# The 15-product expert stage: input sums as a two-step pipeline, six of their steps beside the last triple of products, spaced loads and a new order of the tail

## The chip, the cores and the metric

One core of one Trainium2 chip runs the whole kernel. The metric is the device time of one execution in microseconds, lower is better. TensorE (PE) does the matrix products, VectorE (DVE) and ScalarE (ACT) the elementwise work, GpSimd (POOL) a part of it, and SyncE (SP) issues most of the DMA transfers. Each engine works through its own instructions in program order; semaphores tie them together.

## The reference, cut to what matters

```
for t in range(768):                      # attention, 4 x 8 heads of 48
    y[t]  = r[t] @ (state + (u*k[t]) outer v[t])
    state = w * state + k[t] outer v[t]
x = y as 3072 tokens x 384
h = maximum(maximum(x @ w1, x @ w2), x @ w3);  x = h @ w_out      # 768 wide
rms = sqrt(mean(x*x, axis=-1) + 1e-06);        xn = x / rms * rms_g
g = xn @ w_gate;  val = xn @ w_val                                 # 1536 wide
out = (silu(g) * val) @ moe2_w_out
```

## The kernel before, in words

Tokens are handled as six units of 512. Attention and the first expert layer run unit by unit and fill the first 400 us. The second expert layer, which the change is about, runs as three **passes** p = 0, 1, 2 over pairs of units. Every product in f32 is made of three matmuls on a high part and a low part of each operand (`mm3`, lines 98 to 100: high x high, high x low, low x high), so each operand has to be split: ACT copies the rounded high part, DVE or POOL subtracts it to get the low part.

For gate and value the kernel does not multiply 3 x 3 blocks of weights with 3 blocks of two units directly. It uses a scheme with 15 products on sums and differences of the blocks. The six blocks of a pair of units (a, b, c of the first, d, e, f of the second) are combined into 15 **input sums** by `form_steps(p)`, a generator; one `next` of it is one step. A step makes a sum on DVE (lines 708 and 710) in a buffer of the pool `sb`, splits it with an ACT copy (line 716) and a DVE subtraction (line 717), and leaves the two halves in `sets[i]`. The product i reads `sets[i]`, so the sums of the next pass may overwrite a set once the products of this pass that use it are done. Sums are needed in the order 2, 5, 7, 4, 3, 10, 12, ...

`PLAN` is a table for one **triple** (three of the 12 columns of 128 in the hidden layer): 30 products (`M i x`) and the work around them, with a due time for each. Four copies of it, one period apart, are sorted into one list for each pass, 120 products in all; n counts them. Kinds of entries: `e`, `E` copy a bank to `sb` (line 997), `p`, `c`, `v`, `C` combine banks (lines 999 and 1009), `s` is the Silu (984), `m` the gate times value (988, 990), `h` and `l` split a hidden column into a buffer `hb` (992, 995; there are three such buffers), `o` multiplies it into the output of the pass's first unit (`out_block`, nine matmuls in the three d). The hidden columns of the second unit stay in `h2`; `h_split(f)` splits them (lines 1070, 1071) and `second(f, d)` multiplies them (`b_out`). When an output is complete, `b_out` copies the bank into one of two `ob` buffers and stores it (lines 878, 879).

The order at the end of a pass before: the six `o` blocks that come behind the last product are put between the first blocks of `second`; `form_steps(p + 1)` starts there, one step for each f (and more behind block 20), and what is left of it runs behind the first nine products of the next pass. The last nine blocks of `second` are kept as `filler` for the start of the next pass. In pass 0, `stats_late` sums the squares of the last unit meanwhile.

Beside the products runs the generator `bg` (`behind(p + 1)`), one step per product from n = 25 on: it loads the next pair (`x2_load`, line 696), for the last pair does the Newton steps of 1/rms (lines 539 to 555, small tiles `n`), loads 1/rms to all partitions (`rb`, line 684) and normalises (line 689, six operations). In pass 0 alone every third product also has a weight chunk to make: SP loads three pieces `wsf` (line 650), ACT and POOL split them (655, 656), POOL's queue stores them (657); passes 1 and 2 load the finished chunks (660).

Of the kernel before, what the change touches and what calls it, by code (L numbers as in the profile page):

```python
# [9 lines left out]
F32 = mybir.dt.float32  # L10
F32R = mybir.dt.float32r
# [5 lines left out]
ALU = mybir.AluOpType  # L17
# [48 lines left out]
def r32(ap):  # L66
    return ap.bitcast(F32)
# [3 lines left out]
def rwkv_moe_kernel(ctx, tc, rkT, rkv, wd, ub, cst, rg, w1p, wo1p, w2p, out):  # L71
# [404 lines left out]
    hs, sB = {}, {}  # L476
# [57 lines left out]
    def newton_steps(p, pl):  # L534
        m, y, t = (pl.tile([128, 8], F32, tag=f"n{n}", name=f"n{n}{p}") for n in range(3))
        late = p == NB // 2 - 1
        if late:
            yield
        sync.dma_start(m, msd[p].rearrange("j (a b) -> (j a) b", b=8))
        for _ in range(3):  # L540
            yield
        dve.tensor_scalar(out=m, in0=m, scalar1=1.0 / DM, scalar2=1e-6, op0=ALU.mult, op1=ALU.add)
        dve.tensor_scalar(out=y.bitcast(U32), in0=m.bitcast(U32), scalar1=1, scalar2=0x7fffffff,
                          op0=ALU.logical_shift_right, op1=ALU.bitwise_xor)
        dve.tensor_scalar(out=y, in0=y, scalar1=1.8352577e-20, scalar2=None, op0=ALU.mult)
        dve.tensor_scalar(out=m, in0=m, scalar1=-0.5, scalar2=None, op0=ALU.mult)
        for n in range(4):
            if n == 2:
                yield
            dve.tensor_tensor(out=t, in0=y, in1=m, op=ALU.mult)  # L550
            dve.tensor_tensor(out=t, in0=t, in1=y, op=ALU.mult)
            dve.scalar_tensor_tensor(out=y, in0=t, scalar=1.5, in1=y, op0=ALU.add, op1=ALU.mult)
        if late:
            yield
        sync.dma_start(rsd[p].rearrange("j (a b) -> (j a) b", b=8), y)
# [23 lines left out]
    with tc.manual_schedule():  # L579
# [48 lines left out]
        plan = []  # L628
# [49 lines left out]
        def norm_steps(p):  # L678

            us = (2 * p, 2 * p + 1)  # L680
            x = [x2s.pop(u) for u in us]
            rb = sB["r"].tile([128, 2, 512], F32, tag="rb", name=f"rb{p}")
            for j in range(2):
                sync.dma_start(rb[:, j], rsd[p, j].partition_broadcast(128))
            for _ in range(4 if p else 1):
                yield
            for j in range(2):
                for k in range(3):
                    dve.scalar_tensor_tensor(out=x[j][:, k], in0=x[j][:, k], scalar=rg_sb[:, k:k + 1],
                                             in1=rb[:, j], op0=ALU.mult, op1=ALU.mult)  # L690
                    yield
                xr[us[j]] = x[j]

        def x2_load(u):
# [3 lines left out]
        def form_steps(p):  # L698

            one, two = xr.pop(2 * p), xr.pop(2 * p + 1)  # L700
            a, b, c = (one[:, k] for k in range(3))
            d, e, f = (two[:, k] for k in range(3))
            hold = {}

            def op(name, x, y, kind="add"):
                o = hold[name] = sb.pop(0)
                if kind == "neg":
                    dve.scalar_tensor_tensor(out=o, in0=x, scalar=-1.0, in1=y, op0=ALU.mult, op1=ALU.subtract)
                else:
                    dve.tensor_tensor(out=o, in0=x, in1=y, op=getattr(ALU, kind))  # L710
                return o

            def split(i, x, *drop):
                form_left[0] -= 1
                t = sets[i]
                act.copy(t[:, 0], x)
                dve.tensor_tensor(out=t[:, 1], in0=x, in1=r32(t[:, 0]), op=ALU.subtract)
                for name in drop:
                    sb.append(hold.pop(name))

            s = op("s", e, f, "subtract")
            m = op("m", b, s)
            yield
            split(2, op("t", m, c, "subtract"), "t")
            yield
            split(5, d)
            yield
            w = op("w", a, c, "subtract")
            v = op("v", w, d, "neg")
            yield  # L730
            split(7, op("t", f, v), "t")
            yield
            split(4, v, "v")
            yield
            split(3, op("t", a, d), "t")
            yield
            split(10, w)
            yield
            split(12, op("t", b, a, "subtract"), "t")
            yield  # L740
            split(6, op("t", w, s, "neg"), "t", "w")
            yield
            split(0, s, "s")
            yield
            split(11, op("t", e, d, "subtract"), "t")
            yield
            split(1, m, "m")
            yield
            split(9, f)
            yield  # L750
            split(13, b)
            yield
            split(14, c)
            yield
            split(8, op("t", b, e), "t")

        def set_tiles(t, n):
            for k in range(n):
# [3 lines left out]
        for u in range(NB):  # L762
# [14 lines left out]
            for n, sl in enumerate(slots):  # L777
# [29 lines left out]
                elif u == L:  # L807
                    if n == 0:
                        for v in range(2):
                            x2_load(v)  # L810
                        for _ in range(8):
                            sb.append(br.tile([128, 512], F32, tag="sb", bufs=8, name=f"sb{len(sb)}"))
# [95 lines left out]
        def stats_late():  # L908

            t = [sb.pop(0) for _ in range(3)]  # L910
            for k in range(3):
                sync.dma_start(t[k], x2d[NB - 1, :, k])
            for _ in range(8):
                yield
            for k in range(3):
                act.activation(t[k], t[k], AF.Square)
                if k:
                    pool.tensor_tensor(out=t[0], in0=t[0], in1=t[k], op=ALU.add)
                yield
            yield  # L920
            yield
            sr = br.tile([128, 2, 512], F32R, tag="rb", name="sr")
            hi, lo = sr[:, 0], sr[:, 1]
            act.copy(hi, t[0])
            yield
            dve.tensor_tensor(out=lo, in0=t[0], in1=r32(hi), op=ALU.subtract)
            yield
            yield
            ps = banks.pop(0)
            pe.matmul(ps, ones, hi, start=True, stop=False)  # L930
            pe.matmul(ps, ones, lo, start=False, stop=True)
            act.copy(t[0][0:1], ps[0:1])
            sync.dma_start(msd[NB // 2 - 1, 1:2], t[0][0:1])
            banks.append(ps)
            sb.extend(t)
# [3 lines left out]
        for p in range(NB // 2):  # L939
# [17 lines left out]
            def behind(p):  # L957

                for v in range(2 * p, 2 * p + 2):
                    x2_load(v)  # L960
                yield
                yield
                if p == NB // 2 - 1:
                    yield from newton_steps(p, br)
                yield from norm_steps(p)
# [51 lines left out]
            def out_block(g, f, d):  # L1017
                k = ("h", g, f)
                count[d] += 1
                b_out(3 * g + f, d, get(k), ac, count[d] == 1, count[d] == F2, 2 * p)  # L1020
                drop(k)

            n = 0
            for m, (_, _, kind, g, arg) in enumerate(plan):
                if kind == "M":
# [8 lines left out]
                    drop(("b", g, arg[1], root(arg[0])))  # L1034
                    n += 1
                    if n < 10:
                        next(fs, None)
                    if n >= 25:
                        next(bg, None)
# [13 lines left out]
                elif kind != "o":  # L1053
                    emit(kind, g, arg)
                elif m < last:
                    out_block(g, *arg)
                else:
                    tail.append((arg[0], arg[1], g))
            if more:
# [1 line left out]
            for _ in bg:  # L1061
                pass
            po2 = [banks.pop(0) for _ in range(3)]
            pr = {}
            fs = form_steps(p + 1) if more else iter(())
            late = stats_late() if p == 0 else iter(())

            def h_split(f):
                h = pr[f] = hs_free.pop(0)
                act.copy(h[0], h2[:, f])  # L1070
                dve.tensor_tensor(out=h[1], in0=h2[:, f], in1=r32(h[0]), op=ALU.subtract)  # L1071

            def second(f, d, p=p, po2=po2, pr=pr):
                b_out(f, d, pr[f], po2, f == 0, f == F2 - 1, 2 * p + 1)
                if d == 2:
                    hs_free.append(pr.pop(f))

            tail.sort()
            mix_in = {0: tail[:3], 2: tail[3:]}
            done = 0  # L1080
            for b in range(3 * F2 - (9 if more else 0)):
                f, d = divmod(b, 3)
                while done < F2 and done <= f + 2 and hs_free:
                    h_split(done)
                    done += 1
                second(f, d)
                for f, d, g in mix_in.get(b, ()):
                    out_block(g, f, d)
                next(late, None)
                if d == 0 or b > 20:  # L1090
                    next(fs, None)
            while done < F2:
                h_split(done)
# [185 lines left out]
```

## Time and profile before

| what | value |
|---|---|
| median of 3 runs | 869.72 us (868.94 to 872.7) |
| the profiled execution | 867.82 us, span 866.1 us |
| PE busy | 807.2 us, 93% |
| DVE / ACT / POOL busy | 580.6 / 427.3 / 249.9 us |
| granted TensorE clock, mean | 0.973 |
| chain that ended last | PE 67%, DVE 17%, ACT 6%, DMA 5% |

The span runs from the first to the last instruction of the profiled execution; its own time is 1.7 us longer, and 1.9 us under the median of the runs. Busy PE time is modelled and overlaps, so it does not show stalls well: the distance from one matmul's start to the next does.

### The profile page before, as it was taken

Reading aid. Unit: us, or ns where it says so; the run is one execution under the profiler, and the core shown is the slowest. Engines: PE = TensorE matmul, PEld = TensorE weight load, DVE = VectorE, ACT = ScalarE, POOL = GpSimd, SP = SyncE. Lnnn points to the kernel's source line nnn. Section 1 sums busy time; section 2 is a strip of 40 time slices with the busy share of each in tenths; the row PEclk is TensorE's granted clock in tenths of the full one; section 3 lists DMA queues with packets and bytes.
Section 4 is the critical chain, followed back from the end, with each engine's and each line's share of the span. In section 5 each row is a group of like instructions: output and inputs, shape, how many; then the busy total and the mean of one; then the engine's idle time right before and its main releaser. Section 6 shows DMA issues by size and latency. Waiting matters only on the chain.

```text
span 866.1 us, 14096 instructions
## 1 busy us (share of the span) xinstructions
PE 807.2 (93%) x5098; PEld 657.9 (76%) x5098; DVE 580.6 (67%) x940; ACT 427.3 (49%) x812; POOL 249.9 (29%) x242
## 2 busy tenths in 40 slices
PE   7799999999999999998969998788999879999985
PEld 6688878888888888886848886666788667888864
DVE  6999989688788585187455664766665485655531
ACT  1988955544545532235736663554444345444331
POOL 2588645434445320132646740100000000000000
PEclk8899999999999999999979999989999998999998
DMA  9987677755867541351687754046454304554111
GB/s 247 309 242 236 202 225 222 231 179 145 256 191 230 187 140 30 123 179 64 203 288 235 249 182 143 1 126 228 143 148 146 110 0 144 160 153 146 56 37 40
DMA packets 77898, 142.42 MB, mean 164 GB/s; under 512 B 10486, under 2 KB 40694, under 8 KB 77820
## 3 DMA queue, kind: packets, MB, share of 16 engines
q1 hardware_dynamic: 74476, 125.51, 47.5%
q0 software_dynamic: 3200, 15.73, 4.6%
q8 instruction: 42, 0.69, 0.4%
q14 instruction: 36, 0.29, 0.1%
q10 hardware_dynamic: 144, 0.20, 0.1%
HBM read 101.79 MB, written 35.41 MB: 158 GB/s over the span
## 4 chain that ended last, share of the span: by engine, by line
PE 67%; DVE 17%; ACT 6%; DMA 5%; issue 3%; SPq 1%; POOL 1%; DVEq 0%; ACTq 0%; POOLq 0%
PE px L98 9%; PE px L99 9%; PE px L100 8%; PE pl L98 6%; PE pl L100 6%; PE pl L99 6%; PE pa L98 4%; PE pa L99 4%; PE pa L100 4%; PE py L414 4%; PE pa L356 2%; PE po L99 2%; PE po L100 2%; PE po L98 2%; DMA rb<-rsd 2%
## 5 line engine op out<-in xcount | busy, mean ns | idle before, releaser
L98 PE MATMUL pl<-x,w_a 128*128 128x512 f32 (+1 forms) x342 | 131.9, 386 | 1.7 <-DVE c L499 1.4
L100 PE MATMUL pl<-x,w_a 128*128 128x512 f32 (+1 forms) x342 | 129.5, 379 | 0.7 <-POOL w_a L155 0.7
L99 PE MATMUL pl<-x,w_a 128*128 128x512 f32 (+1 forms) x342 | 129.4, 378 | 0.2 <-DVE x L430 0.2
L98 PEld LDWEIGHTS pl<-x,w_a 128*128 128x128 f32 x342 | 64.3, 188 | 15.4 <-DVE c L499 2.2
L100 PEld LDWEIGHTS pl<-x,w_a 128*128 128x128 f32 x342 | 64.3, 188 | 13.3 <-POOL w_a L155 0.9
L99 PEld LDWEIGHTS pl<-x,w_a 128*128 128x128 f32 x342 | 64.4, 188 | 11.9 <-DVE x L430 0.4
L499 DVE TENSOR_TENSOR c<-pl,c 128x512 f32<-128x512 f32 (+1 forms) x76 | 49.9, 656 | 26.9 <-PE pl L100 24.9
L501 ACT CAST h1h<-c 128x512 fp32r<-128x512 f32 (+1 forms) x32 | 19.0, 594 | 83.5 <-DVE c L499 83.5
L146 DVE SCALAR_TENSOR_TENSOR wf<-wf,wraw 128x384 uint32<-128x384 uint32 x60 | 48.8, 816 | 13.7 <-ACT wraw L139 13.1
L656 POOL TENSOR_TENSOR ws<-wsf,ws 128x384 fp32r<-128x384 f32 x40 | 41.6, 1040 | 54.9 <-ACT ws L655 47.9
L98 PE MATMUL px<-hb,wo 128*128 128x512 f32 x132 | 52.1, 395 | 2.3 <-ACT hb L1070 2.3
L99 PE MATMUL px<-hb,wo 128*128 128x512 f32 x132 | 51.9, 393 | 2.3 <-DVE hb L1071 2.3
L339 POOL TENSOR_SCALAR_AFFINE_SELECT Dg<-a 128x1024 f32<-128x1024 f32 x24 | 30.5, 1269 | 80.9 <-DVE a L336 69.3
L1009 DVE TENSOR_TENSOR px<-px,sb 128x512 f32<-128x512 f32 x46 | 32.1, 699 | 31.9 <-PE px L100 31.4
L100 PE MATMUL px<-hb,wo 128*128 128x512 f32 x132 | 51.4, 390 | 0.0
L997 ACT COPY sb<-px 128x512 f32<-128x512 f32 x53 | 31.1, 587 | 33.3 <-PE px L100 27.1
L363 DVE COPY_PREDICATED Dg<-csb,pa 128x512 f32<-128x512 uint32 x48 | 32.8, 740 | 19.3 <-PE pa L356 16.1
L1071 DVE TENSOR_TENSOR hb<-h,hb 128x512 fp32r<-128x512 f32 x36 | 25.5, 717 | 28.7 <-ACT hb L1070 28.7
L414 PE MATMUL py<-Dg,tm 128*32 128x128 f32 x768 | 41.7, 293 | 0.0
L138 ACT ACTIVATE wraw<-wraw 128x384 uint16<-128x384 uint32 x60 | 38.9, 648 | 1.9
L139 ACT ACTIVATE wraw<-wf 128x384 f16<-128x384 f32 x60 | 38.7, 644 | 1.9
L136 ACT ACTIVATE wf<-wraw 128x384 f32<-128x384 f32 x60 | 33.5, 558 | 12.3 <-DMA w2o<-wf 9.2
(298 smaller groups left out, 2152.9 us busy)
## 6 DMA issues: line engine op xcount, KB each, us to landing
ws<-w2s SPq DMA_DIRECT2D x80, 384.0 KB, 3.0
w2s<-ws POOLq DMA_DIRECT2D x40, 384.0 KB, 3.2
wraw<-in_w2p SPq DMA_DIRECT2D x36, 384.0 KB, 4.9
raw<-in_rkT SPq DMA_DIRECT2D x47, 256.0 KB, 4.1
tm<-in_rkv SPq DMA_DIRECT2D x24, 384.0 KB, 4.5
wsf<-w2f SPq DMA_DIRECT2D x120, 64.0 KB, 2.9
tm<-in_rkv SPq DMA_DIRECT2D x24, 288.0 KB, 5.2
wraw<-in_w1p SPq DMA_DIRECT2D x18, 384.0 KB, 7.9
```

What stands on the lines that cost most here:

```text
L98: pe.matmul(o, lh, rh, start=start, stop=False, **kw)
L99: pe.matmul(o, lh, rl, start=False, stop=False, **kw)
L100: pe.matmul(o, ll, rh, start=False, stop=stop, **kw)
L136: act.activation(w, hi.bitcast(F32), AF.Copy, scale=2.0 ** -112)
L138: act.activation(x[:, :, 0], lo, AF.Copy, scale=2.0 ** -29 * (1 - 2.0 ** -12), bias=-0.4996)
L139: act.activation(x[:, :, 1].bitcast(F16), w, AF.Copy)
L146: dve.scalar_tensor_tensor(out=wu, in0=wu, scalar=3, in1=cbits(n).bitcast(U32), op0=ALU.logical_shift_left, op1=ALU.bitwise_or)
L363: dve.copy_predicated(out=dg[:, :, j], mask=cmask.unsqueeze(1).to_broadcast([128, NP, 128]), data=s["pa"][j])
L414: pe.matmul(o, l, r, start=start, stop=stop)
L499: dve.tensor_tensor(out=c1[:, :n], in0=p[:, :n], in1=c1[:, :n], op=ALU.max)
L656: pool.tensor_tensor(out=t[:, :, 1], in0=r, in1=r32(t[:, :, 0]), op=ALU.subtract)
L1009: dve.tensor_tensor(out=o, in0=a, in1=b, op=op)
```

## The change: what it does

1. `form_steps` becomes a pipeline: a step issues the sum and the ACT copy of its own set, and the DVE subtraction of the set of the step before (`low`, kept in `pend`). The two long-lived values s and w move to a tile of the tag `rb`, the sum of set 1 is made again instead of kept, and the order of sets 7 and 4 is turned. There are 16 steps in place of 17, and one DVE operation more. The pool `sb` gets one buffer more.
2. For passes 0 and 1, `form_steps(p + 1)` is created at n = 100, and a step runs behind the 5th, 7th, 9th, 11th, 13th and 15th of the second unit's products of the last triple (n = 106, 111, 114, 116, 118, 120). The other steps follow in `second`, one for each f and two behind block 24.
3. `behind`: 18 steps instead of 2 lie between the loads of x2 and what follows, 24 instead of 4 between the load of `rb` and the first normalisation, and 3 instead of 1 from one normalisation to the next. The Newton steps of the last pair wait 12 instead of 3 steps for their input, and each iteration is a step.
4. `stats_late`: more steps between the squares, the two parts of the split and the two matmuls; its two tiles come from the tag `ob`.
5. The tail: `h_split(0)` is issued in the plan behind the block `o 0 2` of the last triple; the six late `o` blocks come first, column 2 before column 1, and then `second` in order.

```diff
@@ newton_steps
+        for _ in range(9 if late else 0):
+            yield
...
-            if n == 2:
+            if n == 2 or late:
                 yield
@@ norm_steps
-            for _ in range(4 if p else 1):
+            for _ in range(24 if p else 1):
                 yield
...
                     yield
+                    if p:
+                        yield
+                        yield
@@ form_steps
-            hold = {}
-
-            def op(name, x, y, kind="add"):
-                o = hold[name] = sb.pop(0)
+            keep = sB["r"].tile([128, 2, 512], F32, tag="rb", name=f"rs{p}")
+            s, w = keep[:, 0], keep[:, 1]
+            pend = []
+
+            def op(o, x, y, kind="add"):
...
+            def new(x, y, kind="add"):
+                o = sb.pop(0)
+                op(o, x, y, kind)
                 return o
 
-            def split(i, x, *drop):
+            def low():
+                while pend:
+                    i, x, temp = pend.pop()
+                    t = sets[i]
+                    dve.tensor_tensor(out=t[:, 1], in0=x, in1=r32(t[:, 0]), op=ALU.subtract)
+                    if temp:
+                        sb.append(x)
+
+            def split(i, x, temp=True):
                 form_left[0] -= 1
-                t = sets[i]
-                act.copy(t[:, 0], x)
-                dve.tensor_tensor(out=t[:, 1], in0=x, in1=r32(t[:, 0]), op=ALU.subtract)
-                for name in drop:
-                    sb.append(hold.pop(name))
...
+                act.copy(sets[i][:, 0], x)
+                low()
+                pend.append((i, x, temp))
+
+            op(s, e, f, "subtract")
+            m = new(b, s)
+            op(m, m, c, "subtract")
+            split(2, m)
+            yield
+            op(w, a, c, "subtract")
+            split(5, d, False)
+            yield
+            v = new(w, d, "neg")
+            split(4, v)
+            yield
+            split(7, new(f, v))
+            yield
...
+            split(8, new(b, e))
+            yield
+            low()
@@ stats_late
-            yield
-            yield
-            sr = br.tile([128, 2, 512], F32R, tag="rb", name="sr")
-            hi, lo = sr[:, 0], sr[:, 1]
+            for _ in range(4):
+                yield
+            hi, lo = (br.tile([128, 512], F32R, tag="ob", bufs=2, name=f"sr{n}") for n in range(2))
             act.copy(hi, t[0])
             yield
+            yield
             dve.tensor_tensor(out=lo, in0=t[0], in1=r32(hi), op=ALU.subtract)
-            yield
-            yield
+            for _ in range(4):
+                yield
@@ behind
                 for v in range(2 * p, 2 * p + 2):
                     x2_load(v)
-                yield
-                yield
+                for _ in range(18):
+                    yield
@@ the passes
+                    if n == 100:
+                        fs = form_steps(p + 1) if more else iter(())
+                    if n > 100 and last_m[m] in (5, 7, 9, 11, 13, 15):
+                        next(fs, None)
...
                     out_block(g, *arg)
+                    if g == 3 and arg == [0, 2]:
+                        h_split(0)
...
-            fs = form_steps(p + 1) if more else iter(())
...
-            tail.sort()
-            mix_in = {0: tail[:3], 2: tail[3:]}
-            done = 0
+            for f, d, g in sorted(tail, key=lambda o: (-o[0], o[1])):
+                out_block(g, f, d)
+            done = 1
...
-                for f, d, g in mix_in.get(b, ()):
-                    out_block(g, f, d)
                 next(late, None)
-                if d == 0 or b > 20:
+                if d == 0 or b > 24:
                     next(fs, None)
```

## Rows read from the trace of the kernel before

**Rows 1.** The page, part 1: busy us, share and instructions of each engine.

```profile
PE 807.2 (93%) x5098; PEld 657.9 (76%) x5098; DVE 580.6 (67%) x940; ACT 427.3 (49%) x812; POOL 249.9 (29%) x242
```

**Rows 2.** Stretches of PE: length, busy us (x matmuls touched), granted clock, DMA share, GB/s.

```profile
402.90:412.70 9.80, 6.79 (x28) 1.00 0.00 0
437.70:450.80 13.10, 4.67 (x13) 0.61 0.81 284
480.00:490.00 10.00, 10.00 (x46) 1.00 0.74 232
528.30:531.00 2.70, 1.22 (x5) 1.00 0.44 108
538.50:540.50 2.00, 1.24 (x5) 1.00 0.36 135
547.40:551.40 4.00, 1.18 (x5) 1.00 0.01 2
560.70:570.30 9.60, 4.13 (x11) 0.64 0.12 38
594.30:612.10 17.80, 14.06 (x52) 0.90 0.48 154
680.70:693.00 12.30, 10.04 (x41) 1.00 0.27 96
709.30:720.40 11.10, 5.39 (x14) 0.69 0.12 37
823.80:836.20 12.40, 10.03 (x41) 1.00 0.17 65
```

**Rows 3.** Timeline, 430 to 447 us: start, duration, engine, line [idle before <- releaser].

```profile
430.30 0.91 SPq L696 DMA_DIRECT2D x<-x2d  x2
431.31 2.35 SPq L650 DMA_DIRECT2D wsf<-w2f  x3
434.65 1.20 SPq L684 DMA_DIRECT2D rb<-rsd  x2
...
443.65 0.51 ACT L655 CAST ws<-wsf 128x384 fp32r<-128x384 f32 x1 [6.92 <-DMA wsf<-w2f]
444.07 0.58 ACT L997 COPY sb<-px 128x512 f32<-128x512 f32 x1
...
444.65 1.14 DVE L689 SCALAR_TENSOR_TENSOR x<-x,rg_sb,rb 128x512 f32<-128x512 f32 x1 [8.54 <-DMA rb<-rsd]
...
445.71 0.69 DVE L1009 TENSOR_TENSOR px<-px,sb 128x512 f32<-128x512 f32 x1
```

**Rows 4.** The tile wsf, issues of 431 to 434 us: who waited for it (us, times).

```profile
  ACT ws L655: 6.9, 1
```

**Rows 5.** Timeline at the end of pass 0, 528 to 549 us.

```profile
528.68 0.68 DVE L995 TENSOR_TENSOR hb<-sb,hb 128x512 fp32r<-128x512 f32 x1
...
535.47 0.59 ACT L878 COPY ob<-pa 128x512 f32<-128x512 f32 x1 [1.42 <-PE pa L100]
...
538.22 0.58 ACT L878 COPY ob<-pa 128x512 f32<-128x512 f32 x1 [2.16 <-DMA out<-ob]
...
548.50 0.62 ACT L924 CAST sr<-sb 128x512 fp32r<-128x512 f32 x1 [1.53 <-POOL sb L918]
```

**Rows 6.** Timeline at the start of pass 1, 564 to 567 us.

```profile
564.12 0.62 ACT L716 CAST xw<-sc 128x512 fp32r<-128x512 f32 x1 [1.44 <-DVE sc L710]
...
565.68 0.58 ACT L997 COPY sb<-px 128x512 f32<-128x512 f32 x1
```

**Rows 7.** Timeline in pass 1, at 595 us.

```profile
595.00 0.17 DVE L542 TENSOR_SCALAR n<-n 128x8 f32<-128x8 f32 x1 [2.25 <-DMA n<-msd]
```

**Rows 8.** Stretches, all engines: length, busy of PE, PEld, DVE, ACT, POOL, clock, DMA share, GB/s.

```profile
480.00:505.00 25.00, 25.00 (x111) 20.61 (x110) 15.05 (x23) 16.25 (x32) 16.99 (x23) 1.00 0.71 237
505.00:528.00 23.00, 23.00 (x102) 18.96 (x101) 15.16 (x21) 10.31 (x19) 5.67 (x7) 1.00 0.47 155
```

**Rows 9.** Line 689 in the whole kernel: ns min/median/max, first and last start.

```profile
L689 DVE SCALAR_TENSOR_TENSOR x<-x,rg_sb,rb x18: 736/749/1515, 369.9 to 610.3; 128x512 f32<-128x512 f32 x18
```

More of the change, by code (lines that the diff above doesn't have):

```diff
@@ L710, in op @@
                     dve.tensor_tensor(out=o, in0=x, in1=y, op=getattr(ALU, kind))
-                return o
-            def split(i, x, *drop):
-                form_left[0] -= 1
-                t = sets[i]
-                act.copy(t[:, 0], x)
-                dve.tensor_tensor(out=t[:, 1], in0=x, in1=r32(t[:, 0]), op=ALU.subtract)
-                for name in drop:
-                    sb.append(hold.pop(name))
-            s = op("s", e, f, "subtract")
-            m = op("m", b, s)
+            def new(x, y, kind="add"):
+                o = sb.pop(0)
+                op(o, x, y, kind)
+                return o
@@ L723, in form_steps @@
+            m = new(b, s)
+            op(m, m, c, "subtract")
+            split(2, m)
             yield
-            split(2, op("t", m, c, "subtract"), "t")
+            op(w, a, c, "subtract")
+            split(5, d, False)
             yield
-            split(5, d)
+            v = new(w, d, "neg")
+            split(4, v)
             yield
-            w = op("w", a, c, "subtract")
-            v = op("v", w, d, "neg")
+            split(7, new(f, v))
             yield
-            split(7, op("t", f, v), "t")
+            split(3, new(a, d))
@@ L732, in form_steps @@
             yield
-            split(4, v, "v")
+            split(10, w, False)
             yield
-            split(3, op("t", a, d), "t")
+            split(12, new(b, a, "subtract"))
             yield
-            split(10, w)
+            split(6, new(w, s, "neg"))
             yield
-            split(12, op("t", b, a, "subtract"), "t")
+            split(0, s, False)
             yield
-            split(6, op("t", w, s, "neg"), "t", "w")
+            split(11, new(e, d, "subtract"))
             yield
-            split(0, s, "s")
+            split(1, new(b, s))
@@ L744, in form_steps @@
             yield
-            split(11, op("t", e, d, "subtract"), "t")
+            split(9, f, False)
             yield
-            split(1, m, "m")
+            split(13, b, False)
             yield
-            split(9, f)
+            split(14, c, False)
             yield
-            split(13, b)
+            split(8, new(b, e))
             yield
-            split(14, c)
-            yield
-            split(8, op("t", b, e), "t")
+            low()
         def set_tiles(t, n):
@@ L810, in rwkv_moe_kernel @@
                             x2_load(v)
-                        for _ in range(8):
-                            sb.append(br.tile([128, 512], F32, tag="sb", bufs=8, name=f"sb{len(sb)}"))
+                        for _ in range(9):
+                            sb.append(br.tile([128, 512], F32, tag="sb", bufs=9, name=f"sb{len(sb)}"))
                         set_tiles(ap_.tile([128, 3, 2, 512], F32R, tag="x", bufs=2, name="xa"), 3)
@@ L919, in stats_late @@
                 yield
+            for _ in range(4):
+                yield
+            hi, lo = (br.tile([128, 512], F32R, tag="ob", bufs=2, name=f"sr{n}") for n in range(2))
+            act.copy(hi, t[0])
             yield
             yield
-            sr = br.tile([128, 2, 512], F32R, tag="rb", name="sr")
-            hi, lo = sr[:, 0], sr[:, 1]
-            act.copy(hi, t[0])
-            yield
             dve.tensor_tensor(out=lo, in0=t[0], in1=r32(hi), op=ALU.subtract)
-            yield
-            yield
+            for _ in range(4):
+                yield
             ps = banks.pop(0)
@@ L1021, in out_block, with h_split @@
                 drop(k)
+            last_m, n = {}, 0
+            for m, (_, _, kind, g, arg) in enumerate(plan):
+                if kind == "M":
+                    n += g == 3 and arg[1] == 1
+                    last_m[m] = n if g == 3 and arg[1] == 1 else 0
+            pr = {}
+            def h_split(f, pr=pr):
+                h = pr[f] = hs_free.pop(0)
+                act.copy(h[0], h2[:, f])
+                dve.tensor_tensor(out=h[1], in0=h2[:, f], in1=r32(h[0]), op=ALU.subtract)
             n = 0
@@ L1063, in rwkv_moe_kernel @@
             po2 = [banks.pop(0) for _ in range(3)]
-            pr = {}
-            fs = form_steps(p + 1) if more else iter(())
             late = stats_late() if p == 0 else iter(())
[L1068 to L1071, printed above, removed]
             def second(f, d, p=p, po2=po2, pr=pr):
```

## The prediction, before the changed kernel was run

> **What bounds the kernel now.** I read the page first: PE is busy for 93% of the span [rows 1], so time can only be had where PE stands still, and the question is which of these places the change touches. Then I went through PE's timeline from 400 us on, where the changed stage lies, and listed each place where the distance from one matmul's start to the next exceeds its usual value. Without a stall 44 matmuls start in 10 us (the view of stretches counts 46 touched, two of which began before): 0.227 us each. What a stretch loses is its length less 0.227 us for each matmul in it, always two fewer than the number shown. That gives [rows 2], in order: 3.9 us at the start of pass 0; 10.6 us at 438 us; 2.0, 1.3 and 3.3 us in the tail of pass 0; 7.6 us at the start of pass 1; 6.4 us in its middle; 3.4 us in its tail (a pair of stalls like the first two of pass 0, 2.0 and 1.4); 8.4 us at the start of pass 2; 3.5 us in its tail (the same pair, 2.0 and 1.5). Together 50.4 us. Part of the four long ones is the clock: the granted value in those stretches is 0.61 to 0.90, that is, behind a long stall PE works for a while at the lower of its two levels (1.2 GHz). So a stall that goes takes its slow matmuls with it.
>
> **Starts of passes 1 and 2 (15.9 us).** Before, the last form steps stand in ACT's and DVE's order ahead of the first bank copies of the new pass. A step is a chain: a sum on DVE (0.68 us, as line 995 takes for the same shape [rows 5]), an ACT copy (0.62), a subtraction on DVE (0.68). DVE waits out the copy and ACT the subtraction and the next sum (1.44); the copy `e 2 0` that PE's third product needs ran only at 565.68, behind such pairs [rows 6]. After: six of 16 steps are issued in the last triple, nine at the nine values of f, the last at block 25 of 27. Nothing is left for the new pass. The first copy then waits for its own product and `h_split(11)` alone, and two products and a filler of 0.68 us each lie between. I take 15.5 of the 15.9 us, bounds 11 and 15.9.
>
> **What these six steps cost where they go.** They issue 12 DVE operations (3, 2, 2, 2, 2, 1), 12 x 0.68 = 8.2 us, and six ACT copies, 3.7 us, over products 106 to 120. These are 15 products and 7 `o` blocks of 0.68 us, 15 us. The plan has 15 DVE operations of its own there, 10.2 us, and `h_split(0)` adds one. With 15.2 of 23 us busy before [rows 8], DVE is now overfull. What saves it: the sums depend on nothing recent, so DVE makes them in gaps in which it waited for PE. I followed DVE's order against PE's blocks: entries come 0.4 to 0.8 us late (`c 14`, `p 6`, `c 15`), and what reads them starts 1 us later or more; only the last, `l 2` at the end, has no slack and comes 0.4 us later. I take 1.0 us over both passes, bounds 0 and 6 (0.5 us for each of 12 steps). The additional sum, 0.68 us of DVE per pair, is among the operations counted.
>
> **Middle of pass 1 (6.4 us).** DVE stood at line 542 for the small load of the sums of squares [rows 7], which had been issued right behind the two x2 loads; the six normalisations then came nearly one per product and cost three short stalls. After, the load is issued 19 products after x2 and DVE turns to it 12 products later, over 8 us; the normalisations are 3 products apart. I take 5.8 us, bounds 4 and 6.4.
>
> **The stall at 438 us (10.6 us).** Here I don't follow the obvious reading. DVE waited 8.54 us for `rb`, and `rb` now comes 18 products after x2 and is used 24 later. But ACT waited too, 6.92 us for `wsf`, until 443.65, and the copy on line 997 that PE's chain needs stands behind it at 444.07 [rows 3]. The pieces it waited for were issued at 431.3, just behind the x2 loads, and ahead of `rb` [rows 3, 4]. The change moves neither x2 nor `wsf`. With DVE free, the add on line 1009 starts when the copy ends, 444.65, in place of 445.71. That is 1.0 us, my value. From above the bound is all 10.6 us, if `wsf` was late only because `rb` shared the way.
>
> The Trainium skill (DMA: Bandwidth & Descriptors, section Queues, rings and completion order) says that on each DMA engine descriptors are consumed in ring order. By that, `rb` behind `wsf` cannot hold it up and the gain is the 1.0 us; without it, up to the 10.6 us. The landings (x2, then `wsf` at 443.65, then `rb` at 444.65) agree, but do not exclude the other.
>
> **The tail, first stall (2.0 us in each of three passes).** `second(0, 0)` waited for the two halves of `h_split(0)`, issued behind all else. After, PE goes on with column 2, whose low half (line 995) is ready about 0.3 us after PE wants it; column 1's is next, then 4 us of blocks cover `h_split(0)`. 3 x (2.0 - 0.25) = 5.3 us, bounds 3 and 6.
>
> **The tail, second stall (1.3 to 1.5 us).** It comes from ACT, which waits for the first output's store (2.16 us) to get the `ob` buffer of the third, with `h_split` behind it [rows 5]. The third copy came 2.75 us after the first. After: column 2 takes PE from 528.5 to 530.8, the block `1 0` lets the first copy start at about 531.6, so the third at 534.4; `h_split(1)` has its halves at 535.6 (0.6 + 0.6) and 536.3. PE wants them at 534.9, six blocks behind 530.8. Some 1.4 us are lost again. So 0, bounds -1 and 4.2 for the three.
>
> **Squares' sums (3.3 us).** PE waited for both halves of the split; ACT's copy itself had waited for POOL's adds [rows 5]. After, there are five blocks (3.4 us) between the last square and the copy, then two to the subtraction, five to the matmuls. 3.3 us, bounds 2.5 and 3.3.
>
> **Start of pass 0 (3.9 us).** The same form steps, now without DVE's waits for ACT (0.69 or more each), and with steps 1 and 9 two slots earlier. 3.0 us, bounds 0 and 3.9.
>
> **New costs of spacing.** `rb` (0.5 MB) now enters among `wsf` pieces that have no x2 load in front; a piece behind it may be 3 us late (`rb` is the one load between `wsf` at 443.65 and ACT's free run), against a lead of two chunks, over 4 us. Six normalisations per pass meet a DVE that is 60 to 66% busy [rows 8]; each takes 0.74 to 1.5 us [rows 9], every 2 us or more. I take 0.7 us, bounds 0 and 4.
>
> The Trainium skill (SBUF — State Buffer, section SBUF: two separate sides) speaks against this spacing: a VectorE operation with two SBUF inputs and a GpSimd operation that reads SBUF exclude each other for a whole instruction. Line 689 has two such inputs, and the longest, 1515 ns against a median of 749 [rows 9], fit it. In pass 0 POOL is 68% busy [rows 8], so by the rule six operations could each take 0.75 us longer, 4.5 us of DVE; by the rows alone, under one each. DVE's 9 to 10 idle us in 25 cover either, so neither changes the sum.
>
> **Sum.** 15.5 - 1.0 + 5.8 + 1.0 + 5.3 + 0 + 3.3 + 3.0 - 0.7 = 32.2 us. The profiled execution took 867.8 us (span 866.1, and 1.7 around it), so one like it takes 835.6. The median of the runs shown is 1.9 us higher; I carry the difference along: 837.5 us.
>
> **Rivals.**
> *A, the load wait goes too.* `wsf` lands in time without `rb`. For it: `rb` landed only 1 us behind, so both shared something. Against: order of issue. A further 9.6 us: 827.9 us. Chance 0.15.
> *B, the crowd moves.* DVE, overfull in the last triple and again in the tail (an `h_split` and a form step for each f: 0.7 + 1.2 of 2.04 us, with one ACT copy in between that closes a loop of 2.7 us), comes late, and a third of the start stalls returns as many short ones (5 us), with the upper bounds of crowding and spacing (5 and 3.3 more than I took): 850.8 us at worst, 845 in the middle. For it: DVE's load; against: only five of the nine steps in the tail make a sum, and `h_split` runs two f ahead. Chance 0.21.
> *C, slower.* ACT's copy of a form step blocks ACT in the last triple until DVE has made the sum, and PE's banks wait behind it. It decides where 12 such steps cost over 2.7 us of PE each (32.2 / 12), more than a whole chain of 2.0 us (0.68 + 0.62 + 0.68). At 4 us each: 837.5 + 48 = 885.5 us. Against: the sums run ahead of need. Chance 0.02.
> *D, no change.* The stalls at the starts come not from the form steps but from something as late behind them, and the tail's from the same store: what remains is under 4 us, 866 us or so. Against: rows 6 show the chain itself. Chance 0.02.
>
> **Numbers.** My forecast has a chance of 0.60, and its own range is 831 to 843. The range of 8 in 10 reaches to A below and into B above: 826 to 847; what lies outside is the worse half of B, C, D, and a little beyond A. A run of this kernel can tell about 0.5% (4.3 us) from no change. Faster by more: my forecast, A and B, less a little for what I have not seen, 0.95; within: 0.03; slower: 0.02.
>
> **What would show it.** Right: no gap above 1 us between matmuls at the starts of passes 1 and 2, at the stats matmuls (lines of `stats_late`) or at the Newton steps; no form step's instruction behind the first product of pass 1 or 2; `h_split(0)` ahead of the last `l` on DVE; but still ACT on line 655 waiting some 7 us for `wsf` and a PE gap of 7 us or more there with a low clock, and gaps of about 1 us where `second(1, 0)` begins. Wrong: line 655 without a wait (A); gaps behind DVE or ACT scattered over products 106 to 120 or the tail (B); PE waiting for ACT behind line 716's successor in the last triple (C).

## The result, and the profile after

The changed kernel took 834.84 us (median of 4 runs, 832.82 to 836.63) against 870.4 for the kernel before in the same runs: a ratio of 0.959, interval 0.955 to 0.963. The forecast was 837.5 us, within 826 to 847. The profiled execution has a span of 831.3 us against 866.1, that is 34.8 us less.

The page, part 1, and the row of the TensorE clock over 40 slices:

```profile
PE 798.7 (96%) x5098; PEld 654.6 (79%) x5098; DVE 580.5 (70%) x943; ACT 427.5 (51%) x812; POOL 250.0 (30%) x242
...
PEclk7899999999999999999998999999999999999998
```

The engines do the same work as before [rows 1]; PE waits less. Stretches of PE after the change, in the columns of [rows 2]:

```profile
397.50:408.30 10.80, 10.80 (x47) 1.00 0.11 46
434.70:444.90 10.20, 5.29 (x14) 0.67 0.82 277
520.80:522.20 1.40, 1.18 (x5) 1.00 0.03 7
527.70:529.70 2.00, 1.23 (x5) 1.00 0.47 150
539.20:545.40 6.20, 4.51 (x17) 1.00 0.00 1
546.00:560.00 14.00, 14.00 (x63) 1.00 0.22 57
565.00:600.00 35.00, 35.00 (x155) 1.00 0.65 211
657.40:658.70 1.30, 1.07 (x5) 1.00 0.02 2
664.20:666.20 2.00, 1.22 (x5) 1.00 0.35 131
680.00:700.00 20.00, 20.00 (x89) 1.00 0.40 122
797.00:799.10 2.10, 1.31 (x5) 1.00 0.33 125
```

Here one sees what is gone: the starts of pass 1 (546 to 560) and of pass 2 (680 to 700) run without a gap and at full clock, so does the middle of pass 1 (565 to 600). What is left: a stall at 435 us, still with a clock of 0.67; the first stall of each tail, now 0.7 us in passes 0 and 1 and 0.2 in pass 2; the second one, 1.3 us in all three; and a new one at 540 us. As before I add for all matmuls what lies over 0.227 us from one start to the next, from 380 us on: 51.0 us before, 16.2 after. The difference, 34.8 us, is the whole difference of the spans.

| place, lost us | before | after | saved | forecast |
|---|---|---|---|---|
| starts of passes 1 and 2 | 16.0 | 0 | 16.0 | 15.5, less 1.0 for crowding |
| middle of pass 1 | 6.4 | 0 | 6.4 | 5.8 |
| stall at 438 (now 435) us | 10.6 | 7.4 | 3.2 | 1.0, less 0.7 for spacing |
| first stall of the tails | 6.1 | 1.6 | 4.5 | 5.3 |
| second stall of the tails | 4.1 | 4.0 | 0.1 | 0 |
| squares' sums / late tail of pass 0 | 3.4 | 2.8 | 0.6 | 3.3 |
| start of pass 0 (397 to 413 us) | 4.4 | 0.3 | 4.1 | 3.0 |

The stall at 435 us, in the timeline of the changed kernel (line 657 is 655 of before, 1014 is 997):

```profile
425.79 0.95 SPq L701 DMA_DIRECT2D x<-x2d  x2
...
426.82 2.23 SPq L652 DMA_DIRECT2D wsf<-w2f  x3
...
438.86 0.51 ACT L657 CAST ws<-wsf 128x384 fp32r<-128x384 f32 x1 [5.67 <-DMA wsf<-w2f]
439.27 0.58 ACT L1014 COPY sb<-px 128x512 f32<-128x512 f32 x1
...
439.90 0.80 PE L98 MATMUL px<-xc,ws 128*128 128x512 f32 x1 [4.91 <-ACT sb L1014]
```

DVE has no part in it any more, but ACT still waits for the pieces issued behind x2, and PE for the copy behind that wait. The new stall at 540 us:

```profile
536.28 1.28 POOL L935 TENSOR_TENSOR sb<-sb,sb 128x512 f32<-128x512 f32 x1 [30.56 <-ACT sb L933]
536.30 1.81 DVE L716 TENSOR_TENSOR sb<-x 128x512 f32<-128x512 f32 x1
...
539.44 1.27 POOL L935 TENSOR_TENSOR sb<-sb,sc 128x512 f32<-128x512 f32 x1 [1.89 <-ACT sc L933]
539.84 1.42 DVE L1050 TENSOR_TENSOR hb<-h,hb 128x512 fp32r<-128x512 f32 x1 [1.13 <-ACT hb L1049]
...
541.31 0.50 PE L99 MATMUL px<-hb,wo 128*128 128x512 f32 x1 [0.95 <-DVE hb L1050]
```

Two DVE operations that take 0.69 us elsewhere last 1.81 and 1.42 while POOL adds the squares, and PE waits for the second.

### The profile page after: what moved, and what is told of

It is laid out like the page before. It is cut to its first block, busy times and chain, and to the rows that moved or that the text cites. A ratio compares the mean times of both kernels' runs of the same rounds, so it can differ in the third digit from the quotient of the medians.

```text
span 831.3 us, 14078 instructions
## 1 busy us (share of the span) xinstructions
PE 798.7 (96%) x5098; PEld 654.6 (79%) x5098; DVE 580.5 (70%) x943; ACT 427.5 (51%) x812; POOL 250.0 (30%) x242
## 4 chain that ended last, share of the span: by engine, by line
PE 76%; DVE 10%; ACT 5%; DMA 4%; issue 2%; SPq 1%; POOL 1%; ACTq 0%; DVEq 0%; POOLq 0%
PE px L99 10%; PE px L98 10%; PE px L100 10%; PE pl L98 7%; PE pl L99 6%; PE pl L100 6%; PE pa L99 5%; PE pa L100 5%; PE pa L98 5%; PE py L414 3%; PE pa L356 2%; PE po L99 2%; PE po L100 2%; PE po L98 2%; DVE wf L167 1%
## 5 line engine op out<-in xcount | busy, mean ns | idle before, releaser
L1026 DVE TENSOR_TENSOR px<-px,sb 128x512 f32<-128x512 f32 x51 | 35.5, 699 | 28.4 <-PE px L100 25.7
L1014 ACT COPY sb<-px 128x512 f32<-128x512 f32 x61 | 35.8, 587 | 30.6 <-PE px L100 25.2
L136 ACT ACTIVATE wf<-wraw 128x384 f32<-128x384 f32 x60 | 33.6, 560 | 10.5 <-DMA w2o<-wf 7.2
```

The costliest lines, as they stand in the source:

```text
L136: act.activation(w, hi.bitcast(F32), AF.Copy, scale=2.0 ** -112)
L1014: (act.copy if kind == "e" else dve.tensor_copy)(get(ks[1]), get(ks[0]))
L1026: dve.tensor_tensor(out=o, in0=a, in1=b, op=op)
```

## The experiments

All start from the changed kernel; ratios are to the kernel before, to be held against 0.959. Where a time in us is given as lost, it is summed from the matmuls' starts as above: the first 60 us of the span, where transfers set the pace, differ by several us between executions, and with them the totals (the first product of pass 0 starts at 404.9 us in the profile of the changed kernel and at 412.6 in another with the same work ahead of it). Where a run's interval overlaps that of the changed kernel (0.955 to 0.963), only its trace, of one execution, tells them apart.

**Four parts undone, one at a time.**

Spacing undone:

```diff
-        for _ in range(9 if late else 0):
-            yield
...
-            if n == 2 or late:
+            if n == 2:
...
-            for _ in range(24 if p else 1):
+            for _ in range(4 if p else 1):
...
-                    if p:
-                        yield
-                        yield
...
-                for _ in range(18):
-                    yield
+                yield
+                yield
```

> The changed kernel with its spacing beside the products undone (2 steps behind the x2 loads, 4 behind the rb load, one per normalisation, Newton steps as before). My account: the stretch at 438 us, which the change shortened from 10.6 to 7.4 us, goes back to 10 or 11, and the 6.4 us in the middle of pass 1 return, so 9 to 10 us in all: about 844 us, ratio to the kernel before 0.970. Rival, that these stalls had another cause and went with the form steps: at most 2 us, about 836.

Measured: 845.24 us, ratio 0.972 (0.969 to 0.976). The stall at 434 us is 9.8 us, and 5.7 us are lost in the middle of pass 1 (3.2 and 2.6). Both ends of the 434 us stall are as before: DVE was held 7.84 us for `rb`, ACT 6.29 us for `wsf`. My account holds; in the trace the two places give 8.1 us, a little under the 9 to 10 that I expected.

No step beside the last triple:

```diff
-                    if n == 100:
-                        fs = form_steps(p + 1) if more else iter(())
-                    if n > 100 and last_m[m] in (5, 7, 9, 11, 13, 15):
-                        next(fs, None)
...
+            fs = form_steps(p + 1) if more else iter(())
             late = stats_late() if p == 0 else iter(())
```

> The changed kernel with no form step beside the last triple: all 16 start in the tail, the rest falls behind the first products of the next pass. My account, that the stalls at the starts of passes 1 and 2 (7.6 and 8.4 us before) come from form steps in front of the first bank copies: five steps are left there, both stalls return, shortened by the pipeline to 3 to 7 us each with their slow clock, 841 to 848 us. Rival, that the two-step pipeline alone removes them: gaps under 1 us at both starts, 835 us or less.

Measured: 848.97 us, ratio 0.975 (0.972 to 0.977). Stretches of PE at the end and the start of the passes:

```profile
537.70:547.00 9.30, 6.80 (x21) 0.82 0.00 1
554.10:564.10 10.00, 7.01 (x18) 0.66 0.12 39
695.00:703.90 8.90, 4.45 (x13) 0.81 0.15 44
```

The first is in the tail of pass 0, where 5.0 us are lost in place of 2.8. The other two are the starts: both lose 6.4 us, with a low granted clock (0.66, 0.81). With the pipeline alone the starts would be only 1 to 2 us better than before [rows 2]. The place of the six steps is what removes the stalls.

Pipeline undone, places kept:

```diff
                 act.copy(sets[i][:, 0], x)
-                low()
                 pend.append((i, x, temp))
+                low()
```

> The changed kernel with each set's subtraction made in its own step again (DVE waits for ACT's copy), all places of the steps as in the change. My account, that the place of the steps is what counts: both starts stay without a gap, the tails of passes 0 and 1 lose 0 to 3 us each where h_split comes late, the start of pass 0 loses 1 to 3 us: 836 to 841 us. Rival, that the pipeline carries the gain: the waits on ACT, 0.7 us for each of 15 sets, come back in full on PE, 10 us for each of the two pairs and some at the start of pass 0, 855 us or more.

Measured: 846.9 us, ratio 0.972 (0.970 to 0.975); both accounts missed. The starts of passes 1 and 2 stay without a gap, as mine had it. But 5.6 us are lost at the start of pass 0 (0.3 with the pipeline), and in the last triple and the first tail stall 3.7 us in each pass (0.7 with it):

```profile
397.60:411.60 14.00, 9.87 (x40) 1.00 0.26 98
516.90:518.40 1.50, 0.69 (x4) 1.00 0.72 231
525.60:534.30 8.70, 7.48 (x29) 1.00 0.33 98
```

So the pipeline is what lets DVE take the six steps there: without it DVE waits 0.69 us for ACT's copy in four of the six steps (516 to 531 us), and PE's waits up to 532 us all end with the plan's own operations on DVE (line 1026), which stand behind those.

Old order of the tail:

```diff
-                    if g == 3 and arg == [0, 2]:
-                        h_split(0)
...
-            for f, d, g in sorted(tail, key=lambda o: (-o[0], o[1])):
-                out_block(g, f, d)
-            done = 1
+            tail.sort()
+            mix_in = {0: tail[:3], 2: tail[3:]}
+            done = 0
...
+                for f, d, g in mix_in.get(b, ()):
+                    out_block(g, f, d)
```

> The changed kernel with the old order of the tail (h_split(0) behind the plan, late o blocks between the first blocks of second). My account: the first stall of each tail goes back from 0.2 to 0.7 to 2.0 us, the second stays at 1.3, so 4 to 5 us: 839 us. Rival, that the form steps already made beside the triple leave DVE and ACT free and the old order costs nothing now: 835 us.

Measured: 844.87 us, ratio 0.971 (0.967 to 0.975). The first stall is 3.1, 5.9 and 2.0 us in the three tails: in passes 0 and 1 longer than the 2.0 us of the kernel before. That makes 9.4 us more in all, twice the 4 to 5 that I expected. The timeline in pass 1 shows why:

```profile
660.93 0.61 ACT L733 CAST xb<-rs 128x512 fp32r<-128x512 f32 x1
...
661.45 0.61 ACT L1049 CAST hb<-h 128x512 fp32r<-128x512 f32 x1
...
662.12 0.51 PE L98 MATMUL pa<-hb,wo 128*128 128x512 f32 x1 [1.53 <-ACT hb L1049]
...
663.61 0.79 PE L99 MATMUL pa<-hb,wo 128*128 128x512 f32 x1 [0.98 <-DVE hb L1050]
```

The last form step beside the triple (line 733) stands ahead of `h_split(0)` (1049). Moving steps there without a new tail would have cost the tail more; the two parts need each other.

**The squares' sums.** The spacing of the sums alone undone (the tiles stay in `ob`):

```diff
-            for _ in range(4):
-                yield
+            yield
+            yield
...
             act.copy(hi, t[0])
             yield
-            yield
...
-            for _ in range(4):
-                yield
+            yield
+            yield
```

> The changed kernel with the spacing of the squares' sums as before the change (2 blocks to the copy, 1 to the subtraction, 2 to the matmuls; tiles still in ob). My account, that the spacing saved most of the 3.3 us that PE stood at these two matmuls: 2 to 3 us return, 837 us. Rival, that the new tail order and DVE's lighter load there had already done it: 835 us.

Measured: 840.66 us, ratio 0.965 (0.960 to 0.970). 6.6 us are lost from 543 to 553 us in place of 2.8, of which PE waited 4.22 at the first matmul for the ACT copy. In the trace the spacing is worth 3.8 us, more than the 3.3 that the kernel before lost.

Adds on DVE in place of POOL:

```diff
-                    pool.tensor_tensor(out=t[0], in0=t[0], in1=t[k], op=ALU.add)
+                    dve.tensor_tensor(out=t[0], in0=t[0], in1=t[k], op=ALU.add)
```

> The changed kernel with the two adds of the squares on DVE in place of POOL. In the tail of pass 0 a DVE sum took 1.81 us and a subtraction 1.42, in place of 0.69, while POOL added, and PE lost 2.7 us there. If POOL's adds hold up DVE: those two operations take 0.69 us again and the gap shrinks to 1 us or less, about 833 us. Rival, that DVE has too much to do there in any case: two more operations make the gap as long or longer, 835 to 837 us.

Measured: 832.2 us, ratio 0.956 (0.952 to 0.960). The same two operations, with the adds on DVE:

```profile
535.98 0.68 DVE L935 TENSOR_TENSOR sb<-sb,sb 128x512 f32<-128x512 f32 x1
536.58 0.69 DVE L716 TENSOR_TENSOR sb<-x 128x512 f32<-128x512 f32 x1
...
538.49 0.69 DVE L935 TENSOR_TENSOR sb<-sb,sc 128x512 f32<-128x512 f32 x1 [0.62 <-ACT sc L933]
539.10 0.68 DVE L1050 TENSOR_TENSOR hb<-h,hb 128x512 fp32r<-128x512 f32 x1
```

Both last 0.69 us again; two adds on DVE cost less than two on POOL. The stall shrinks from 2.8 to 1.6 us, not to under 1. The rest is the load that the squares' sums put on ACT and DVE: the tail of pass 1, which has the same steps without them, keeps only its two short stalls (PE loses 2.0 us in all from 655 to 680 us in the changed kernel).

**What was left of the tail.** `h_split(1)` ahead of the copies of the first outputs:

```diff
                 out_block(g, f, d)
-            done = 1
+                if f == 2 and d == 2:
+                    h_split(1)
+            done = 2
```

> The changed kernel with h_split(1) issued right behind the three late o blocks of column 2, ahead of the copies of the first outputs. My account, that the second stall of each tail (1.3 us) is ACT waiting for a store to free an ob buffer with h_split(1) behind it: all three go, 3 to 4 us less, 831 us. Rival, that h_split(1) is late because of its own buffer or DVE: no change, 835 us.

Measured: 831.27 us, ratio 0.954 (0.950 to 0.958). No second stall is left in any pass, 4.0 us less; the stall at 540 us grew from 2.8 to 3.9, so 2.5 us net in the trace.

**The x2 loads.** In pass 0 in six pieces, one every six products (the last pair, in pass 1, keeps its two loads):

```diff
-                    x2_load(v)
-                for _ in range(18):
-                    yield
...
+                        x2s[v] = br.tile([128, 3, 512], F32, tag="x2", bufs=2, name=f"x2_{v}")
+                        for k in range(3):
+                            sync.dma_start(x2s[v][:, k], x2d[v, :, k])
+                            for _ in range(6):
+                                yield
```

> The changed kernel with the x2 loads of pass 0 cut into six pieces of 256 KB, one every six products, in place of two loads of 768 KB back to back. My account, that ACT waits for wsf pieces which stand behind the 1.5 MB of x2: the wait of line 657 at 439 us and the PE gap of 7.4 us with its slow clock go, down to 1 us or less: 827 to 828 us. Rival, that the transfers as a whole are too many there (277 GB/s in that stretch): the gap breaks into several smaller ones, 832 to 836 us.

Measured: 827.47 us, ratio 0.949 (0.945 to 0.952). PE runs from 430 to 500 us without a gap:

```profile
430.00:500.00 70.00, 70.00 (x308) 1.00 0.85 289
```

How long the small `wsf` pieces take to land there, from the view of the tile `wsf`, issues of 433 to 460 us:

```profile
DMA to landing us min/median/max: 3.4/4.0/5.0
```

The gain is what I expected, but the run cannot tell order from amount: the pieces of x2 are smaller and also spread over more time. The next one keeps the bytes and the moment and changes the queue:

```diff
-            sync.dma_start(x2s[u], x2d[u])
+            act.dma_start(x2s[u], x2d[u])
```

> The changed kernel with the x2 loads issued from ACT's queue in place of SP's, same place, same bytes. My account, that wsf is late because it stands behind x2 in the same queue: ACT's wait on line 657 and the PE gap of 7.4 us go or shrink to 2 us or less: 827 to 830 us. Rival, that x2's bytes crowd wsf out whatever queue they come from: the gap stays at 5 us or more, 833 to 836 us.

Measured: 836.43 us, ratio 0.961 (0.957 to 0.965); my account falls. PE loses 0.7 and 6.1 us. The view of the tile `wsf`, issues of 434.4 to 437 us:

```profile
L652 SPq DMA_DIRECT2D wsf<-w2f x3: 442/812/1147, 434.5 to 435.8; - x3
...
  ACT ws L657: 3.6, 1
...
DMA to landing us min/median/max: 11.0/11.4/11.9
```

The pieces stand in SP's queue, x2 in ACT's, and still they land after 11.0 to 11.9 us, as late as behind x2 in one queue (in the changed kernel the pieces issued from 426.8 to 428.3 us let ACT go on at 438.86, 10.5 to 12 us later). So the order in one queue is not what makes them late. What this run and the changed kernel have in common with the kernel before is 1.5 MB at once on top of the pass's own transfers: in the 14 us from the loads on the transfers move 306 to 310 GB/s in both and both stall, while with the pieces 334 GB/s pass for 30 us and PE loses nothing:

```profile
433.00:463.00 30.00, 30.00 (x133) 24.70 (x132) 21.01 (x29) 21.44 (x43) 22.90 (x30) 1.00 0.98 334
```

So it is not the load over the stretch, but what is issued at once, that makes single small transfers wait. Whether the size of one load counts or that several come back to back was not tested.

**Edits together.** Pieces, `h_split(1)` early and adds on DVE, the three diffs above in one kernel:

> The three edits together: x2 in pieces, h_split(1) early, the squares' adds on DVE. If each account holds they add up, 7 + 4 + 2 us: 822 us. If only the loads account holds: 828. If none: 835.

Measured: 823.1 us, ratio 0.946 (0.942 to 0.949); the three add up nearly as expected. From 410 to 513 us and from 537 to 640 PE has no gap. Two kinds of stall are left: 0.7 us in the first one of the tails of passes 0 and 1, and 2.1 us at 531 to 537, in the tail of pass 0, where PE waits for splits on ACT and DVE. To take that load away, the squares' sums were then moved whole behind the first products of pass 1 (one `next(late)` for each product, where each block of `second` had one):

```diff
+        late = stats_late()
         for p in range(NB // 2):
...
+                    if p == 1:
+                        next(late, None)
                     if n < 10:
                         next(fs, None)
...
-            late = stats_late() if p == 0 else iter(())
...
-                next(late, None)
...
-            for _ in late:
-                pass
```

> The three edits (x2 in pieces, h_split(1) early, squares' adds on DVE) and the squares' sums moved out of the tail of pass 0, one step behind each of the first products of pass 1. If the 2.1 us that the three edits left in the tail of pass 0 come from the sums of squares on a DVE that is full there: they go, no gap over 1 us is left behind 400 us, 821 us. Rival, that they return at the start of pass 1, where DVE and ACT carry the bank copies: 823 us or more.

> As the run with four edits, but the two adds of the squares on POOL again, now beside the first products of pass 1. If POOL's adds hold up DVE wherever they stand: one or two DVE operations at the start of pass 1 stretch to 1.4 to 1.8 us; DVE has idle time there, so PE loses under 1 us, 821 to 822 us. Rival, that the stretch reaches PE: 823 us or more.

Measured: 821.78 us with the adds on DVE, ratio 0.945 (0.941 to 0.949), and 821.61 us with the adds on POOL, ratio 0.945 (0.942 to 0.949). The three versions can't be told apart by their ratios; in the traces the loss from 380 us on falls from 4.7 to 3.1 and 2.6 us. The 2.1 us are gone; at the start of pass 1 PE loses 0.6 us with the adds on DVE and nothing with those on POOL. My expectation for POOL was wrong in its mechanism: no DVE operation got longer.

```profile
553.03 1.29 POOL L935 TENSOR_TENSOR sb<-sb,sc 128x512 f32<-128x512 f32 x1 [1.24 <-ACT sc L933]
553.09 0.70 DVE L1035 TENSOR_TENSOR px<-px,sb 128x512 f32<-128x512 f32 x1 [1.35 <-PE px L100]
```

This DVE operation, which reads one operand from a PSUM bank (`px`, where PE puts its products), runs its usual 0.70 us beside POOL's add. The two that were stretched at 540 us read both operands from SBUF. One operation shows little, but the trace of the changed kernel has more of them. I counted DVE's TENSOR_TENSOR operations on 128x512 from 380 us on. With an input in PSUM, 39 ran for over 0.1 us beside one of POOL's TENSOR_TENSOR operations, and none took over 0.70 us. With both inputs in SBUF, 15 did: ten took 0.91 to 2.27 us, five 0.68 to 0.69. The 137 that ran without one took 0.67 to 0.70.

Both versions beat the changed kernel by some 13 us, and the kernel before by 50 (0.945 against 0.959 and 1).

## Why the prediction was right, and where a term was not

The likeliest case came true: 837.5 forecast, 834.84 measured, and the sum of 32.2 us stands against 34.8 in the trace. Rivals A to D did not happen as a whole, but a part of B did, in the tail of pass 0. That the sum lies nearer than some of its terms is luck: 2.2 us too little at 438 us and 2.7 too much at the squares' sums nearly cancel.

**Starts of the passes.** Right in mechanism and size (15.5 and 16.0 us). The run without the steps beside the triple shows that their place is the cause. **The cost beside the triple** was put at 1.0 us and is what the first tail stall keeps, 0.7 us in each of passes 0 and 1 against 0.2 in pass 2, which has no such steps, so 0.9 us: `l 2` has no slack, as worked out. What the prediction did not work out is that this holds only with the pipeline; without it 3.7 us are lost there.

**Middle of pass 1.** Right (5.8 and 6.4); undoing the spacing brings 5.7 us back. The cost of the spacing, put at 0.7 us, did not appear: among the spaced normalisations, from 446 to 519 and from 560 to 655 us, PE loses less than 0.1 us. The idle time of DVE set against it was 8.5 to 10 us in 25 by [rows 8], not 9 to 10, which changes nothing.

**The stall at 438 us.** Right that ACT's wait for `wsf` would hold PE although DVE became free; it did, 5.67 us. The term was mis-sized: 1.0 forecast, 3.2 measured. I let PE stop at the same product as before and only took DVE's tail off. But the product at which PE stopped before was itself waiting for DVE. From the x2 loads to the stop PE now runs 8.8 us (425.8 to 434.6), before 7.3 (430.3 to 437.6). That is 1.5 of the 2.2 us missing, about two blocks of 0.68 us. At the other end, PE now starts 0.05 us behind ACT's copy (439.85 and 439.90); the forecast had kept the DVE add of 0.69 us between the two, which PE waited for before. That is 0.7 us more, and ACT's wait ends 0.3 us sooner after the loads; 0.4 us more of matmuls at the low clock goes off again.

The reason I gave for the rest was too narrow: "issued at 431.3, just behind the x2 loads". If the order in one queue had made `wsf` late, it would have come through once x2 was in another. The run with x2 on ACT's queue shows landings of 11.0 to 11.9 us all the same. The rule I had set beside my reason (the Trainium skill, DMA: Bandwidth & Descriptors, Queues, rings and completion order: descriptors are consumed in ring order on each DMA engine) is not at odds with that: it speaks of the order in one ring, not of a load in another. The conclusion, that `rb` was not the cause, holds; that the order in the queue was, does not. How the engines share out such a burst stays open.

**Tails.** First stall 5.3 forecast, 4.5 measured; the difference is the cost beside the triple, which the forecast counted by itself. Second stall: right that the new order leaves it at 1.3 to 1.4 us, and `h_split(1)` ahead of the copies takes it away, as an `ob` copy in front of it was the cause.

**Squares' sums.** The step that failed: "3.3 us, bounds 2.5 and 3.3". PE hardly waits at the two matmuls any more, but 2.8 us are lost around them, so 0.6 was saved. I had the rule at hand that says why in part (the Trainium skill, SBUF — State Buffer, SBUF: two separate sides: a VectorE operation with two SBUF inputs and a GpSimd operation that reads SBUF exclude each other) and applied it to the normalisations alone, where DVE had idle time. POOL's two adds of the squares fall into a stretch where DVE has little. The trace agrees with the rule in both directions: 1.81 and 1.42 us in place of 0.69 with both inputs in SBUF, 0.70 unchanged with one in PSUM. With the adds on DVE 1.2 of the 2.8 us go; the other 1.6 are the load of the sums in that stretch, which went when they were moved out of it. The timeline of the kernel before had shown such stretched operations already, at the same two adds:

```profile
545.50 1.29 POOL L918 TENSOR_TENSOR sb<-sb,sd 128x512 f32<-128x512 f32 x1 [32.29 <-ACT sd L916]
...
545.96 1.38 DVE L717 TENSOR_TENSOR xa<-x,xa 128x512 fp32r<-128x512 f32 x1 [0.35 <-ACT xa L716]
...
546.87 1.60 POOL L918 TENSOR_TENSOR sb<-sb,sb 128x512 f32<-128x512 f32 x1
...
547.26 1.75 DVE L1071 TENSOR_TENSOR hb<-h,hb 128x512 fp32r<-128x512 f32 x1
```

**Start of pass 0.** 3.0 forecast, 4.1 saved: the pipeline takes out all waits of DVE for the form steps' copies there. A stall of 0.6 us at 398 us, which [rows 2] leave out, puts it above the bound of 3.9. Without the pipeline 5.6 us are lost.

## What to carry to other kernels

A stall that two engines hold up goes only in part when one is freed; look for every wait that ends near it, and ask at which instruction the stalled engine will stop next. Moving work into another stage needs both a place and a form in which the engines don't wait for each other: here neither the place (6.4 us lost at each start without it) nor the pipeline (3.7 us in each pass without it) would have been enough alone. Spread a large load over the products instead of issuing it at once, even where the transfers have room on average.

## What of the hardware was not expected

Moving the x2 loads to another engine's queue did not let small transfers pass: they landed after 11.0 to 11.9 us as in the same queue, though the transfers ran at 310 GB/s, while at 334 GB/s, with the same load in six portions, they landed after 3.4 to 5.0 us and PE lost nothing. And a POOL add of 1.28 us made a DVE operation of 0.69 us last 1.81, nearly the 1.26 us that were left of the add and its own 0.69; with an operand in PSUM none of 39 operations of this kind took longer than 0.70.
